# The last supertile's PSUM copies in two pairs of banks, each pair with a store of its own

## The chip, the cores and the metric

One core of a Trainium2 chip. The metric is the device time of one execution in microseconds (us), lower is better. Beside it I use the span of a profiled execution, which is 1.7 us shorter than its time wherever both are on record, and the **tail**: the end of the span minus the start of ScalarE's first copy of the last supertile. Tails are worked out from the trace's records, which carry more digits than the page. Engine names in the profile: PE is TensorE, DVE is VectorE, ACT is ScalarE, SPq is SyncE's queue. PSUM is the memory that TensorE writes its sums to; a bank is here one of the four parts of 512 numbers that the kernel's tile `ps` has in each partition. SBUF holds the other tiles. A packet is a piece that one of the 16 DMA engines moves at a time, and the backlog is what earlier stores have left for them to do.

## The reference

A depthwise convolution with a 1x1 kernel is a scaling of the channels; the pointwise convolution behind it is a matrix product.

```python
# x: (1, 384, 384, 384), dw: (1, 1, 384), pw: (384, 384), all bfloat16
out = x * dw[0, 0]
return einsum('bhwc,cd->bhwd', out, pw)
```

So it is a product of 147,456 x 384 by 384 x 384, with 113 MB read and 113 MB written.

## The kernel before

The rows are worked through in 288 supertiles of 512 rows. VectorE transposes a supertile, TensorE multiplies it into four PSUM banks, ScalarE copies the banks to an output tile in bfloat16, SyncE stores the tile in chunks of up to 10 supertiles. Towards the end the chunks get small: 4, 2, 1 and 1 supertiles.

```python
    head, tail = [[1, 1, 2, 2, 4]], [[6, 4], [4, 2, 1, 1]]
    ...
        def store(t):
            ...
            else:
                dst = rows.rearrange("(m q) d -> m (q d)", q=4)
            nc.sync.wait_ge(s_a[je % 2], je // 2 + 2)
            if je + 1 == NS:
                nc.sync.wait_ge(s_d, 1)
            nc.sync.dma_start(dst, src).then_inc(s_o[g % NR], 16)
    ...
            nq = 4
            if jj + 1 == NS:
                nq = 2
                nc.vector.wait_ge(s_o[g % NR], 16 * sum(map(len, groups[g % NR : g : NR])))
                e = nc.vector.tensor_copy(Ov[:, nq:4, j, :], PS[s][:, nq:4, :D])
                e._wait_ge(s_pe, 2 * jj + 2)
                e.then_inc(s_d)
            a = nc.scalar.copy(Ov[:, 0:nq, j, :], PS[s][:, 0:nq, :D])
            a._wait_ge(s_pe, 2 * jj + 2)
            a.then_inc(s_a[s])
```

In the last supertile alone VectorE, which has nothing left to transpose, copies banks 2 and 3 while ScalarE copies 0 and 1. One store of 393,216 bytes follows; each partition writes 3072 consecutive bytes.

## Time and profile before

| | before |
|---|---|
| time, median of 3 runs | 575.4 us (575.3 to 575.55) |
| span of the profiled run | 573.39 us |
| start of the last supertile's copies | 568.67 us |
| tail | 4.72 us |

TensorE is busy for 99% of the span, and one supertile takes it 1.95 us. The only part that this change can reach is the tail: two copies, one store, its landing, the program's end. The prediction below shows the lines and how to read them. What one does with the tail: take the times of the last copies and of SyncE's issue from the timeline, then look at the DMA share in slices of 0.1 us, to see whether the DMA engines wait for the store or the store for them.

### The profile page before, as it was taken

What the parts mean: (1) busy time and instruction counts of PE and PEld (TensorE: products, weight loads), DVE (VectorE), ACT (ScalarE), POOL (GpSimd) and SP (SyncE); (2) the same over time, 40 slices, a digit from 0 to 9 for tenths busy, and PEclk for the clock granted to TensorE, in tenths of its full rate; (3) what the DMA queues carried; (4) which work ended last, traced back from release to release, by engine and by line L of the source; (5) the groups of instructions that cost most, each with busy time, mean ns of one, the idle gap of its engine ahead of it and who ended that gap; (6) DMA issues with size and microseconds to landing.
All of it is one profiled execution on the core that took longest, in us unless ns stands there. A gap on an engine that the chain in (4) does not pass through costs nothing.

```text
span 573.4 us, 29717 instructions
## 1 busy us (share of the span) xinstructions
PE 566.5 (99%) x13869; PEld 414.7 (72%) x13869; DVE 506.7 (88%) x583; ACT 419.0 (73%) x296; POOL 0.9 (0%) x8
## 2 busy tenths in 40 slices
PE   8999999999999999999999999999999999999996
PEld 5777777777777777777777777777777777777774
DVE  7898889889889888988988988898898898889884
ACT  6777777777777777777777777777777777777775
POOL 0000000000000000000000000000000000000000
PEclk9999999999999999999999999999999999999999
DMA  9999999999999999999999999999999999998676
GB/s 363 420 340 434 417 425 432 445 414 422 428 414 425 387 400 427 392 408 390 430 392 385 404 425 401 396 416 421 399 392 411 418 387 393 422 401 364 267 288 233
DMA packets 25253, 226.88 MB, mean 396 GB/s; under 512 B 1178, under 2 KB 5147, under 8 KB 21403
## 3 DMA queue, kind: packets, MB, share of 16 engines
q1 hardware_dynamic: 24064, 225.61, 97.0%
q10 hardware_dynamic: 1178, 1.18, 0.6%
q14 instruction: 10, 0.07, 0.0%
q8 instruction: 1, 0.02, 0.0%
HBM read 113.54 MB, written 113.25 MB: 396 GB/s over the span
## 4 chain that ended last, share of the span: by engine, by line
PE 99%; ACT 0%; DVE 0%; issue 0%; POOL 0%; POOLq 0%; SPq 0%
PE ps L183 98%; PE ps L200 0%; ACT w_r L289 0%; DVE O L322 0%; PE ps L233 0%; POOL zero L249 0%; POOL warm L248 0%; PE ps L215 0%; POOLq L358 0%; SPq L103 0%
## 5 line engine op out<-in xcount | busy, mean ns | idle before, releaser
L183 PE MATMUL ps<-w_r,T 32*128 32x384 bf16 x13824 | 561.8, 321 | 0.7 <-ACT w_r L289 0.7
L276 DVE STREAM_TRANSPOSE T<-X 128x384 uint32<-128x384 uint32 x572 | 500.0, 876 | 56.0 <-DMA X<-in_x_dram 0.3
L325 ACT CAST O<-ps 128x1536 bf16<-128x1536 f32 x288 | 413.8, 1437 | 147.6 <-PE ps L183 147.6
L183 PEld LDWEIGHTS ps<-w_r,T 32*128 32x128 bf16 x13824 | 412.9, 93 | 149.4 <-issue 0.9
L289 ACT CAST w_r<-ps 128x768 bf16<-128x768 f32 x5 | 3.6, 818 | 1.0 <-PE ps L233 1.0
L200 PE MATMUL ps<-zero 32*128 32x384 bf16 x24 | 2.6, 494 | 1.4 <-POOL zero L249 1.4
L276 DVE STREAM_TRANSPOSE T<-Xl 128x384 uint32<-128x384 uint32 x4 | 3.5, 876 | 0.4
L322 DVE CAST O<-ps 128x768 bf16<-128x768 f32 x1 | 1.0, 958 | 3.0 <-PE ps L183 3.0
L261 ACT ACT_TABLE_LOAD x1 | 1.3, 1283 | 1.9 <-issue 1.9
L200 PEld LDWEIGHTS ps<-zero 32*128 32x128 bf16 x24 | 0.7, 99 | 2.6 <-issue 2.6
L233 PE MATMUL ps<-pw_n,sel_w 64*128 64x384 bf16 x18 | 2.2, 403 | 0.0
L233 PEld LDWEIGHTS ps<-pw_n,sel_w 64*128 64x128 bf16 x18 | 1.0, 114 | 1.3 <-issue 0.7
L294 DVE TENSOR_REDUCE sel<-eye 128x64 f32<-128x128 bf16 x1 | 0.3, 290 | 1.8 <-POOL eye L251 1.8
L289 DVE CAST w_r<-ps 128x768 bf16<-128x768 f32 x1 | 1.0, 958 | 0.9 <-PE ps L233 0.9
L304 DVE TENSOR_SCALAR sel_w<-sel,dw_f 128x256 bf16<-128x256 f32 x3 | 0.9, 350 | 0.0
L301 DVE COPY dw_f<-ps 128x3 f32<-128x3 f32 x1 | 0.2, 160 | 0.8 <-PE ps L215 0.8
L215 PEld LDWEIGHTS ps<-ones,dw_row 1*128 1x128 bf16 x3 | 0.2, 100 | 0.2 <-issue 0.2
L251 POOL TENSOR_SCALAR_AFFINE_SELECT eye<-ones 128x128 bf16<-128x128 bf16 x1 | 0.3, 292 | 0.1
L261 ACT COPY warm<-warm 128x1 f32<-128x1 f32 x2 | 0.3, 188 | 0.0
L249 POOL MEMSET zero<- 128x192 uint32 x1 | 0.3, 258 | 0.0
L215 PE MATMUL ps<-ones,dw_row 1*128 1x1 bf16 x3 | 0.2, 160 | 0.0
L250 POOL MEMSET ones<- 128x128 bf16 x1 | 0.2, 204 | 0.0
(5 smaller groups left out, 0.5 us busy)
## 6 DMA issues: line engine op xcount, KB each, us to landing
X<-in_x_dram SPq DMA_DIRECT2D x26, 3840.0 KB, 21.8
out_dram<-O SPq DMA_DIRECT2D x26, 3840.0 KB, 27.4
X<-in_x_dram SPq DMA_DIRECT2D x3, 1536.0 KB, 18.3
out_dram<-O SPq DMA_DIRECT2D x3, 1536.0 KB, 8.1
X<-in_x_dram SPq DMA_DIRECT2D x3, 768.0 KB, 7.2
out_dram<-O SPq DMA_DIRECT2D x3, 768.0 KB, 12.9
X<-in_x_dram SPq DMA_DIRECT2D x1, 2304.0 KB, 19.9
out_dram<-O SPq DMA_DIRECT2D x1, 2304.0 KB, 11.7
```

The source lines that it names most:

```text
L183: mm = nc.tensor.matmul(PS[s][:, q, :D], lhsT=Ts[s][32 * q : 32 * q + 32, b, par::2], rhs=w_r[32 * q : 32 * q + 32, b, par, :], start=(b, ...
L200: nc.tensor.matmul(PS[0][:, i, :D], lhsT=zero[32 * i : 32 * i + 32, 0:P], rhs=zero[32 * i : 32 * i + 32, :], start=True, stop=True, tile_p ...
L215: mm = nc.tensor.matmul(PS[1][:, 0, D + k : D + k + 1], lhsT=dw_row[:, P * k : P * k + P], rhs=ones[0:1, 0:1], start=True, stop=True,)
L233: mm = nc.tensor.matmul(PS[(k + 1) % 2][:, 2 * r + v, :D], lhsT=sel_w[64 * v : 64 * v + 64, k, r, :, :].rearrange("p q w -> p (q w)"), rhs ...
L249: nc.gpsimd.memset(zero[:].bitcast(U32), 0).then_inc(s_zero)
L251: nc.gpsimd.affine_select(out=eye[:], in_=ones[:], pattern=[[-1, P]], compare_op=mybir.AluOpType.is_equal, fill=0.0, base=0, channel_multi ...
L261: c = nc.scalar.copy(warm[:, s + 1 : s + 2], warm[:, 0:1])
L276: ins = nc.vector.transpose(out=Tw[:, 3 * h : 3 * h + 3], in_=Xw[:, :, j, 96 * h : 96 * h + 96].rearrange("p k (b w) -> p b k w", w=32),)
L289: o = nc.vector.tensor_copy(out, in_) if e == 0 else nc.scalar.copy(out, in_)
L304: nc.vector.tensor_scalar_mul(sel_w[:, k], sel[:].unsqueeze(2).to_broadcast([P, 2, 4, 32]), dw_f[:, k : k + 1]).then_inc(s_sw)
L322: e = nc.vector.tensor_copy(Ov[:, nq:4, j, :], PS[s][:, nq:4, :D])
L325: a = nc.scalar.copy(Ov[:, 0:nq, j, :], PS[s][:, 0:nq, :D])
```

## The change

Its intent: get the first half of the last supertile on its way before the second half has been copied.

```diff
+            if je + 1 == NS:
+                for k in range(2):
+                    part = slice(2 * D * k, 2 * D * k + 2 * D)
+                    nc.sync.wait_ge(s_a[je % 2], je // 2 + 2 + k)
+                    nc.sync.wait_ge(s_d, k + 1)
+                    nc.sync.dma_start(dst[:, part], src[:, part]).then_inc(s_o[g % NR], 16)
+                return
             nc.sync.wait_ge(s_a[je % 2], je // 2 + 2)
-            if je + 1 == NS:
-                nc.sync.wait_ge(s_d, 1)
             nc.sync.dma_start(dst, src).then_inc(s_o[g % NR], 16)
 ...
-            nq = 4
             if jj + 1 == NS:
-                nq = 2
                 nc.vector.wait_ge(s_o[g % NR], 16 * sum(map(len, groups[g % NR : g : NR])))
-                e = nc.vector.tensor_copy(Ov[:, nq:4, j, :], PS[s][:, nq:4, :D])
-                e._wait_ge(s_pe, 2 * jj + 2)
-                e.then_inc(s_d)
-            a = nc.scalar.copy(Ov[:, 0:nq, j, :], PS[s][:, 0:nq, :D])
+                nc.vector.wait_ge(s_pe, 2 * jj + 2)
+                nc.scalar.wait_ge(s_pe, 2 * jj + 2)
+                for q in (0, 2):
+                    nc.scalar.copy(Ov[:, q, j, :], PS[s][:, q, :D]).then_inc(s_a[s])
+                    nc.vector.tensor_copy(Ov[:, q + 1, j, :], PS[s][:, q + 1, :D]).then_inc(s_d)
+                continue
+            a = nc.scalar.copy(Ov[:, :, j, :], PS[s][:, :, :D])
```

(Cut: the final wait counts one store more.)

## The prediction

> **What bounds the kernel now.** I read four views in this order: the page (what is busy over the whole span), the chain of work that ended last, the timeline of the last five microseconds, and the DMA traffic in slices of a tenth of a microsecond there. The change touches only the last of 288 supertiles, so everything turns on what follows the last matmul.
>
> From the page, busy times and the by-engine shares of the chain:
>
> ```profile
> PE 566.5 (99%) x13869; PEld 414.7 (72%) x13869; DVE 506.7 (88%) x583; ACT 419.0 (73%) x296; POOL 0.9 (0%) x8
> PE 99%; ACT 0%; DVE 0%; issue 0%; POOL 0%; POOLq 0%; SPq 0%
> ```
>
> TensorE is busy for 99% of the span. The chain in order of time (start, length, what) ends so:
>
> ```profile
> 6.84 561.80 PE ps L183 x13824
> 568.65 0.02 issue
> 568.67 0.96 DVE O L322
> ```
>
> The matmuls run without a break from 6.84 to 568.65 us, and the changed lines touch none of their operands before the last supertile. The span ends at 573.4, so 573.39 - 568.65 = 4.74 us lie behind the last matmul. That is 0.8% of 575.4: if the change removed the whole tail it would still not be 2%. The tail on the timeline (start, length), then SyncE's own waits from 568 us on:
>
> ```profile
> 568.67 0.80 ACT L325 CAST O<-ps 128x768 bf16<-128x768 f32 x1 [0.51 <-PE ps L183]
> 568.67 0.96 DVE L322 CAST O<-ps 128x768 bf16<-128x768 f32 x1 [3.02 <-PE ps L183]
> 569.72 0.34 SPq L139 DMA_DIRECT2D out_dram<-O  x1
> ...
> SPq L158 <- DMA out_dram<-O: 2.0, 1, 2.0
> SPq L139 <- ACT O L325: 1.6, 1, 1.6
> ```
>
> The two copies start together; VectorE ends last, at 569.63. SyncE issues the store at 569.72, 0.09 us later, and is done with issuing at 570.06. It then waits 2.0 us for the landing, until about 572.1; the remaining 1.3 us to 573.4 is the program's end, which no part of the change touches. What are the DMA engines doing meanwhile? Columns: stretch, length, five engines' busy times, TensorE clock, DMA share, GB/s.
>
> ```profile
> 570.20:570.30 0.10, 0.00 (x0) 0.00 (x0) 0.00 (x0) 0.00 (x0) 0.00 (x0) 1.00 0.99 399
> 570.30:570.40 0.10, 0.00 (x0) 0.00 (x0) 0.00 (x0) 0.00 (x0) 0.00 (x0) 1.00 0.28 93
> 570.40:570.50 0.10, 0.00 (x0) 0.00 (x0) 0.00 (x0) 0.00 (x0) 0.00 (x0) 1.00 0.03 0
> 570.50:570.60 0.10, 0.00 (x0) 0.00 (x0) 0.00 (x0) 0.00 (x0) 0.00 (x0) 1.00 0.56 215
> 570.60:570.70 0.10, 0.00 (x0) 0.00 (x0) 0.00 (x0) 0.00 (x0) 0.00 (x0) 1.00 0.96 369
> ...
> 571.50:571.60 0.10, 0.00 (x0) 0.00 (x0) 0.00 (x0) 0.00 (x0) 0.00 (x0) 1.00 0.49 185
> 571.60:571.70 0.10, 0.00 (x0) 0.00 (x0) 0.00 (x0) 0.00 (x0) 0.00 (x0) 1.00 0.04 0
> ```
>
> This is the view that decides. Until 570.3 the DMA engines are still full with the store of the supertile before (a backlog: two earlier stores kept them at about full share from 563.5 on). Then there is a hole, then the last store runs at full rate until about 571.6. The hole is (1 - 0.28) + (1 - 0.03) + (1 - 0.56) = 1.73 slices of 0.1 us, so **0.17 us**. The first bytes of the last store move some 0.8 us after its issue began at 569.72. So the last store's start is set by the copies, but only just: had it been issued 0.2 us earlier, it would have stood in line behind the backlog.
>
> **What the Trainium skill says.** "DMA: Bandwidth & Descriptors", section "Latency and other measured facts": about 600 ns to the first byte for a transfer issued from SyncE or ScalarE. The trace has 0.8 us from the start of the issue, of which 0.34 is the issue itself; I use 0.84. The same page, section "Queues, rings and completion order": on each DMA engine descriptors of one issuer's ring are consumed in ring order. Both halves and the store before them come from SyncE, so an early half can at best follow the backlog without a hole. "VectorE: DVE Perf Modes", section on the TRN2 errata: from PSUM a copy of FD elements costs 120 + FD cycles at 0.96 GHz on VectorE and 172 + FD at 1.2 GHz on ScalarE, 525 and 463 ns for 384. The trace's own rows decide below and come out slightly longer. "PSUM — Partial Sum Buffer", section on bank collisions: two engines may read at once if their banks differ. Before and after, ScalarE and VectorE always hold different banks (0 and 1, then 2 and 3, of the four), so I expect neither an error nor a slowdown; the trace shows both copies at the durations that they have elsewhere.
>
> **The change part by part.** The matmuls, the other 287 supertiles and the order of instructions there stay; the listing of instructions per engine shows only two 384-wide copies for one 768-wide on ScalarE and on VectorE, and two stores for one.
>
> *Copies.* ScalarE took 1439 ns for 1536 elements and 799 for 768: 640/768 = 0.833 ns an element and 159 ns fixed, so 384 take 479 ns. VectorE took 958 for 768 and 160 for three elements from PSUM (the tiny copy of dw_f), so 1.04 an element and 157 fixed: 384 take 557 ns. Copies of one engine overlap by their fixed part: the three 348 ns VectorE operations of 256 elements at the start of the kernel fill 0.88 us, a pitch of (0.88 - 0.35)/2 = 0.265, and ScalarE's three weight copies fill 2.21 us at 817 each, a pitch of 0.70 for 768 elements, so 0.06 above the pure element time. So the second pair starts 0.40 (VectorE) and 0.38 (ScalarE) after the first. The wait for the matmuls is now an instruction of its own; I give it 0.03 us. First pair done: 568.70 + 0.56 = 569.26. Second: 568.70 + 0.40 + 0.56 = 569.66, against 569.63 before.
>
> *Stores.* Half A is issued at 569.26 + 0.09 = 569.35, 0.37 us earlier than the one store. SyncE is busy with it for 0.34, to 569.69, which is just when the second pair ends; with two waits of about 0.05 each, half B is issued near 569.80, 0.08 us later than the one store was. With 0.84 us of lead, A could move from 570.19 and B from 570.64.
>
> *DMA engines.* At 570.19 they still hold the backlog, so A follows it directly at about 570.4. The hole of 0.17 us is gone. A's 196,608 bytes take about 0.5 us, to 570.9, so B (ready at 570.64) follows A without a hole too. But the halves go in runs of 1536 bytes a partition instead of 3072. The trace has both sizes: the store of the next-to-last chunk but one moved in 1536-byte runs, the one after it in 3072:
>
> ```profile
> 567.30:569.30 2.00, 1.33 (x35) 0.72 (x24) 0.63 (x1) 1.49 (x2) 0.00 (x0) 1.00 1.04 377
> ...
> 569.50:570.30 0.80, 0.00 (x0) 0.00 (x0) 0.13 (x1) 0.00 (x0) 0.00 (x0) 1.00 0.99 396
> ```
>
> 393,216 bytes take 1.043 us at 377 GB/s and 0.993 at 396: **0.05 us** lost.
>
> *Sum.* -0.17 (hole) + 0.05 (shorter runs) = **-0.12 us** on the end of the last byte; landing (last byte to the end of SyncE's wait, some 0.4 us) and program end are as before. The 0.37 us by which A is earlier mostly goes into standing behind the backlog. Time: 575.4 - 0.12, about 575.3.
>
> **The rivals.** First, the full intent: nothing stands in front of half A, and the last byte follows B's issue only. B ready at 570.64 plus 0.52 us of bytes gives 571.16 instead of 571.6, so -0.45 us, 574.95. Against it speaks the full DMA share up to 570.3. Second, half B's issue becomes the end: if issuing two stores back to back cost more than the 0.34 us seen, or the waits on two semaphores did, B might only start at 571.1, after a new hole; then the end is 571.1 + 0.52 = 571.6, no gain, 575.4. Against it: SyncE's consecutive issues in the trace are 344 and 345 ns long. To get worse than before by even 0.3 us B would have to be issued at 570.4, 0.7 us after A's issue ended. Third, the backlog itself shifts by chance, since stores before it drain a little faster or slower against other traffic; that alone moves the hole between 0 and about 0.3 us and would hide the effect. None of the rivals reaches a per cent.
>
> **Range and chances.** Three runs before spread over 0.25 us, and executions of one kernel otherwise agree within 0.3%. An effect of -0.12 us (0.02%) is under the spread. I predict 575.3 us; the range, 574.8 to 575.8, takes the full intent less a little at the bottom and a set of runs 0.4 us slower at the top. Within 2%: 0.99. Faster and slower by over 2% need something that the tail of 4.74 us cannot give, and get 0.005 each.
>
> **What would show it.** Right: four 384-wide copies of 0.48 and 0.56 us, the pairs ending near 569.26 and 569.66 us; two SyncE issues about 0.45 us apart, the first at 569.35; no hole in the DMA share around 570.4; the last byte near 571.5 and SyncE's last wait shorter than 2.0 us (about 1.8, as it also starts 0.08 later). Wrong: a hole before half A (then the backlog was not what held it), a hole between A and B (the second rival), matmuls that end at a time other than 568.65 us by over 0.2 us (then something outside the tail moved), or a time outside 574.8 to 575.8.

## The result, and the profile after

| | before | after |
|---|---|---|
| time, median of 4 runs | 575.41 us (575.30 to 575.55) | 575.15 us (574.97 to 575.58) |
| ratio | 1 | 0.9996, interval 0.9982 to 1.0010 |
| span of the profiled run | 573.39 us | 573.86 us |
| start of the last copies | 568.67 us | 569.29 us |
| tail | 4.72 us | 4.58 us |

A ratio is the mean time of one kernel's fast runs over that of the other's of the same rounds, so not quite the ratio of the medians.

By the time the change is within noise. The profile tells more, and at first sight contradicts: the profiled run of the changed kernel has the longer span. The table says why: its tail is 0.14 us shorter, but its last copies start 0.61 us later (by the records' further digits). That lateness does not come from the tail, nor from the loop. Following ScalarE's output copies through both traces, the first one starts at 9.02 us before and at 9.64 after, and the difference is 0.61 us at the first, at the 97th and at the 277th supertile. The whole 0.61 us arose before the first supertile was finished, in code that the change does not touch. So I compare tails, and come back to the start in the last experiment.

The timeline of the tail after (start, length), then SyncE's waits in it:

```profile
569.29 0.86 ACT L329 CAST O<-ps 128x384 bf16<-128x384 f32 x2 [0.51 <-PE ps L189]
569.36 1.02 DVE L330 CAST O<-ps 128x384 bf16<-128x384 f32 x2 [3.09 <-PE ps L189]
570.00 0.85 SPq L141 DMA_DIRECT2D out_dram<-O  x2
...
SPq L164 <- DMA out_dram<-O: 1.7, 1, 1.7
SPq L144 <- ACT O L332: 1.6, 1, 1.6
SPq L140 <- DVE O L330: 0.8, 1, 0.8
```

The first store is issued 0.71 us after the copies' start (570.00 - 569.29), against 1.05 before (569.72 - 568.67); the second, by the trace's records, 1.17 us after it. SyncE's last wait is 1.7 us instead of 2.0. The DMA share in the stretch that answers to the hole before (0.61 us later), and at the end of the last store:

```profile
570.80:570.90 0.10, 0.00 (x0) 0.00 (x0) 0.00 (x0) 0.00 (x0) 0.00 (x0) 1.00 1.06 430
570.90:571.00 0.10, 0.00 (x0) 0.00 (x0) 0.00 (x0) 0.00 (x0) 0.00 (x0) 1.00 0.78 292
571.00:571.10 0.10, 0.00 (x0) 0.00 (x0) 0.00 (x0) 0.00 (x0) 0.00 (x0) 1.00 1.11 384
571.10:571.20 0.10, 0.00 (x0) 0.00 (x0) 0.00 (x0) 0.00 (x0) 0.00 (x0) 1.00 0.91 323
571.20:571.30 0.10, 0.00 (x0) 0.00 (x0) 0.00 (x0) 0.00 (x0) 0.00 (x0) 1.00 1.11 399
...
572.00:572.10 0.10, 0.00 (x0) 0.00 (x0) 0.00 (x0) 0.00 (x0) 0.00 (x0) 1.00 0.46 154
572.10:572.20 0.10, 0.00 (x0) 0.00 (x0) 0.00 (x0) 0.00 (x0) 0.00 (x0) 1.00 0.02 0
```

The share scatters about 1 (a packet is booked in the slice where it starts, so single slices read above and below), but there is no hole: both halves follow the backlog without a gap. The last byte has moved 2.87 us after the copies' start, against 3.01 before; from there to the end it is 1.70 us in both.

### The profile page after: what moved, and what is told of

Same layout as the page of the kernel before. It is cut to its first block, busy times and chain, and to the rows that moved or that the text cites. A ratio compares the mean times of both kernels' runs of the same rounds, so it can differ in the third digit from the quotient of the medians.

```text
span 573.9 us, 29721 instructions
## 1 busy us (share of the span) xinstructions
PE 567.8 (99%) x13869; PEld 383.5 (67%) x13869; DVE 508.0 (89%) x584; ACT 419.1 (73%) x297; POOL 0.9 (0%) x8
## 3 DMA queue, kind: packets, MB, share of 16 engines
q10 hardware_dynamic: 1178, 1.18, 0.6%
## 4 chain that ended last, share of the span: by engine, by line
PE 99%; DVE 0%; issue 0%; POOL 0%; POOLq 0%; DVEq 0%; SPq 0%
PE ps L189 98%; PE ps L239 1%; PE ps L206 0%; DVE O L330 0%; POOL zero L255 0%; POOL warm L254 0%; PE ps L221 0%; POOLq L365 0%; DVEq L326 0%; SPq L103 0%
## 5 line engine op out<-in xcount | busy, mean ns | idle before, releaser
L189 PEld LDWEIGHTS ps<-w_r,T 32*128 32x128 bf16 x13824 | 381.5, 93 | 181.0 <-issue 0.7
```

The source lines that it names most:

```text
L189: mm = nc.tensor.matmul(PS[s][:, q, :D], lhsT=Ts[s][32 * q : 32 * q + 32, b, par::2], rhs=w_r[32 * q : 32 * q + 32, b, par, :], start=(b, ...
```

## The experiments

My theory: the hole ahead of the last store is what the change closes, for the price of shorter runs. The rivals: the tail scatters by chance; the split copies themselves save time; two transfers are faster than one. Times without a ratio come from single runs, whose state is unknown; tails are compared across them because the loop keeps its pace of 1.95 us a supertile in every trace looked at and the tail repeats, as the first two runs show. In the diffs, `-` and `+` are against the changed kernel unless said otherwise.

**1 and 2. Both kernels once more, unedited.**

> The kernel before, unedited, to learn how far a profile repeats. I measure the tail: end of the span minus the start of ScalarE's last copy (of the first one, where there are two). Before 4.72 us, after 4.58. Theory (hole): the tail is set by the store queue, so it repeats within 0.05 us: 4.67 to 4.77, with a hole in the DMA share of about 0.17 us ahead of the last store; the span differs from 573.39 only by what happens ahead of the first supertile, up to 0.6 us. Rival (backlog by chance): the earlier stores drain differently each time, and the tail scatters by 0.15 us or more, so that the 0.14 us between before and after could be chance.

> The changed kernel, unedited. Theory (hole): tail 4.53 to 4.63 us again, no hole in the DMA share, and the pace of the loop, one supertile in 1.95 us, is as before; in the time a ratio of 0.9995 to 1.0000. Rival (chance): a tail anywhere from 4.5 to 4.8. Second rival (the copies got quicker or slower): the second pair of copies ends at a place other than 1.10 us after the start of the first.

Measured: tails 4.72 and 4.57 us; so each repeats within 0.005 us, and chance is out (a third pair, in experiments 11 and 12 and on another chip, agrees). The span of the kernel before was 0.97 us longer than in the first profile, more than the 0.6 allowed for, and all of it had arisen before the first output copy (9.99 us against 9.02). The second pair of copies ends 1.09 us after the start of the first, as in the first profile. But the times: 576.08 (one run) for the kernel before, and for the changed kernel 575.25, median of 5 (575.05 to 575.61), against 575.21, median of 9, ratio 1.0001 (0.9988 to 1.0015), where 0.9995 to 1.0000 was expected. A saving of 0.14 us is 0.02%, and the times scatter by 0.5 us.

**3. The split copies with one store.**

```diff
-                for k in range(2):
-                    part = slice(2 * D * k, 2 * D * k + 2 * D)
-                    nc.sync.wait_ge(s_a[je % 2], je // 2 + 2 + k)
-                    nc.sync.wait_ge(s_d, k + 1)
-                    nc.sync.dma_start(dst[:, part], src[:, part]).then_inc(s_o[g % NR], 16)
+                nc.sync.wait_ge(s_a[je % 2], je // 2 + 3)
+                nc.sync.wait_ge(s_d, 2)
+                nc.sync.dma_start(dst, src).then_inc(s_o[g % NR], 16)
```

(Cut: the final wait counts one store less again.)

> The four copies of the change, but one store as before, after all four. Theory (hole): the store is issued about 1.18 us after the copies' start instead of 1.05, because two copies on one engine end later than one; the hole grows by as much to about 0.3 us, tail 4.85 us (4.80 to 4.90), worse than both kernels. Rival (the copies are what saves): 4.58 as in the changed kernel.

Measured: tail 4.85 us (time of the one run 575.74). Issue at 570.36, 1.18 us after the copies' start:

```profile
569.18 0.86 ACT L327 CAST O<-ps 128x384 bf16<-128x384 f32 x2 [0.51 <-PE ps L187]
...
570.36 0.34 SPq L139 DMA_DIRECT2D out_dram<-O  x1
```

The hole, in the same columns as before:

```profile
570.80:570.90 0.10, 0.00 (x0) 0.00 (x0) 0.00 (x0) 0.00 (x0) 0.00 (x0) 1.00 0.28 93
570.90:571.00 0.10, 0.00 (x0) 0.00 (x0) 0.00 (x0) 0.00 (x0) 0.00 (x0) 1.00 0.03 0
571.00:571.10 0.10, 0.00 (x0) 0.00 (x0) 0.00 (x0) 0.00 (x0) 0.00 (x0) 1.00 0.00 0
571.10:571.20 0.10, 0.00 (x0) 0.00 (x0) 0.00 (x0) 0.00 (x0) 0.00 (x0) 1.00 0.08 31
571.20:571.30 0.10, 0.00 (x0) 0.00 (x0) 0.00 (x0) 0.00 (x0) 0.00 (x0) 1.00 0.96 369
```

It is one slice and a bit longer than before, and the tail is 0.13 us longer, which is the delay of the issue (1.18 - 1.05). With a hole ahead of it, the start of the last store follows its issue one for one. The split copies alone cost time.

**4. The copies of before with two stores**, ScalarE's half first.

```diff
-                    nc.sync.wait_ge(s_a[je % 2], je // 2 + 2 + k)
-                    nc.sync.wait_ge(s_d, k + 1)
+                    if k == 0:
+                        nc.sync.wait_ge(s_a[je % 2], je // 2 + 2)
+                    else:
+                        nc.sync.wait_ge(s_d, 1)
...
-                for q in (0, 2):
-                    nc.scalar.copy(Ov[:, q, j, :], PS[s][:, q, :D]).then_inc(s_a[s])
-                    nc.vector.tensor_copy(Ov[:, q + 1, j, :], PS[s][:, q + 1, :D]).then_inc(s_d)
+                nc.scalar.copy(Ov[:, 0:2, j, :], PS[s][:, 0:2, :D]).then_inc(s_a[s])
+                nc.vector.tensor_copy(Ov[:, 2:4, j, :], PS[s][:, 2:4, :D]).then_inc(s_d)
```

> The two copies of before (ScalarE banks 0 and 1, VectorE 2 and 3), but two stores: the first after ScalarE's copy alone, the second after VectorE's. Theory (hole): the first half is issued about 0.9 us after the copies' start and can move 0.84 us later, at 1.73, as the backlog ends (1.65 to 1.80), so the hole closes all but some hundredths: tail 4.57 to 4.65. Then the splitting of the copies bought nothing. Rival (the early pair is needed): the first half comes after the backlog's end with a hole of 0.1 us or more, tail 4.68 to 4.72.

Measured: tail 4.59 us (575.0 for the one run). The first half is issued 0.82 us after the copies' start instead of 0.71, and of the hole one slice of 0.66 is left:

```profile
570.20:570.30 0.10, 0.00 (x0) 0.00 (x0) 0.00 (x0) 0.00 (x0) 0.00 (x0) 1.00 1.01 399
570.30:570.40 0.10, 0.00 (x0) 0.00 (x0) 0.00 (x0) 0.00 (x0) 0.00 (x0) 1.00 0.66 231
570.40:570.50 0.10, 0.00 (x0) 0.00 (x0) 0.00 (x0) 0.00 (x0) 0.00 (x0) 1.00 1.06 369
```

So of the 0.14 us, 0.12 come from the second store alone; pairing the banks adds 0.02, no more than the moment of the last byte varies among the three profiles with the changed ending (2.87 to 2.90 us after the copies' start, 2.89 here). ScalarE's half ends earlier than VectorE's anyway, and that was head start enough.

**5. Two stores, both held until all four copies are done.**

```diff
-                    nc.sync.wait_ge(s_a[je % 2], je // 2 + 2 + k)
-                    nc.sync.wait_ge(s_d, k + 1)
+                    nc.sync.wait_ge(s_a[je % 2], je // 2 + 3)
+                    nc.sync.wait_ge(s_d, 2)
```

> The change's copies and two stores, but both stores wait for all four copies. Tail measured as end of the span minus the start of ScalarE's first copy of the last supertile; one store after four copies had 4.85 us. Theory (the saving is the early issue of the first half, and halves themselves cost a little): the first half is issued 1.18 us after the copies' start, moves from about 2.02, the second follows without a hole, and the run of two times eight short packets an engine takes 0.05 us more than eight long ones: tail 4.86 to 4.92. Rival (two transfers are quicker by themselves): below 4.82.

Measured: tail 4.93 us (575.52), a little over the range. The first issue lies 1.18 us after the copies' start, the same as in experiment 3, so the two differ only in one store against two halves: **0.085 us is the price of the halves**. Two transfers are not faster by themselves. The two lines to set beside those of experiment 3:

```profile
568.87 0.86 ACT L329 CAST O<-ps 128x384 bf16<-128x384 f32 x2 [0.51 <-PE ps L189]
...
570.05 0.82 SPq L141 DMA_DIRECT2D out_dram<-O  x2
```

By the trace's records a 3072-byte packet takes about 0.124 us on its DMA engine and a 1536-byte one 0.067, more than half. The last supertile's 8 or 16 packets an engine so take 8 x 0.124 = 0.99 or 16 x 0.067 = 1.07 us, which is nearly all of it.

**6 to 8. A shorter backlog.** The last supertiles are grouped 2, 2, 2, 1, 1 instead of 4, 2, 1, 1, so that the earlier stores start sooner. Done to the kernel before, to the changed kernel, and to experiment 4:

```diff
-    head, tail = [[1, 1, 2, 2, 4]], [[6, 4], [4, 2, 1, 1]]
+    head, tail = [[1, 1, 2, 2, 4]], [[6, 4], [2, 2, 2, 1, 1]]
```

> The kernel before with the last supertiles grouped 2, 2, 2, 1, 1 instead of 4, 2, 1, 1, so that the store queue is some 0.2 to 0.3 us less behind when the last store comes. Theory (the last store is started by its own issue): tail 4.72 us as before, only the hole ahead of it grows to 0.3 us or more. Rival (the backlog holds the last store in the kernel before as well): tail 4.45 to 4.6.

> The changed kernel with the same grouping. Theory (in the changed kernel the backlog holds the first half, by 0.1 to 0.25 us): both halves move earlier, the first from about 1.55 us after the copies' start, the last byte about 0.25 us earlier than in the changed kernel: tail 4.28 to 4.38, thus 0.35 to 0.4 less than the kernel before. In the time: 0.9990 to 1.0000, as the start of the kernel scatters by up to a microsecond. Rival (half B's own issue, 1.17 us after the copies' start, already sets the end): tail 4.55 to 4.6.

> The two unsplit copies with two stores (ScalarE's half first), with the same grouping. Theory (splitting the copies is worth nothing behind the backlog and 0.1 us without it, as the first half is issued 0.87 instead of 0.76 us after the last matmul): tail 4.40 to 4.46, about 0.1 more than with split copies. Rival (something later sets the end in both): equal within 0.03.

Measured: tails 4.69, 4.48 and 4.57 us. For the first two the direction is the theory's: the kernel before hardly moves (its store starts with its own issue), the changed kernel gains 0.10 us (its first half stood behind the backlog). Of these gains 0.02 and 0.03 us lie behind the last byte, though, from which it is 1.68 us to the end here instead of 1.70; the last byte itself comes 0.01 us earlier in the kernel before and 0.07 in the changed one. The sizes of the last two were missed, 4.28 to 4.38 and 4.40 to 4.46 being expected. For the changed kernel the reason is the backlog: I had expected it to end 0.2 to 0.3 us sooner, and by the trace's records its last packet ended only 0.06 to 0.09 us sooner (1.72 to 1.74 us after the copies' start instead of 1.78 to 1.82). For experiment 4 it is not: its last byte does not come earlier at all (2.91 us after the copies' start, 2.89 before), because its first half, issued at 0.82 us, had only just reached the backlog and now has a hole ahead of it again. The 0.10 us between split and unsplit copies came as expected. Time of the changed kernel so grouped: 575.13, median of 6, against 575.25, ratio 0.9998 (0.9985 to 1.0010). The other two, single runs: 575.79 and 575.23.

**9 and 10. Hardly any backlog left**: the same with 2, 2, 1, 1, 1, 1, for the changed kernel and for experiment 4.

> The changed kernel with the last supertiles grouped 2, 2, 1, 1, 1, 1, so that the store queue is empty earlier: the grouping 2, 2, 2, 1, 1 freed it only 0.09 us earlier and brought a tail of 4.48 us where I had expected 4.28 to 4.38. Theory (the backlog holds the first half until about 1.6 us after the copies' start, then its own issue does, 0.71 + 0.84): a little hole ahead of the first half; the last byte about 1.2 us after that, tail 4.40 to 4.48. Rival (no backlog at all is worth what my prediction called the full intent): tail 4.2 to 4.3.

> The unsplit copies with two stores, ScalarE's half first, with the grouping 2, 2, 1, 1, 1, 1. Theory (without a backlog the tail follows the issue of the first half, 0.11 us later than with split copies): tail 0.08 to 0.14 us above that of tail1_after. Rival: equal within 0.03.

Measured: tails 4.46 and 4.54 us (575.25 and 575.08, single runs). Now the first half of the changed kernel has a hole ahead of it again:

```profile
570.30:570.40 0.10, 0.00 (x0) 0.00 (x0) 0.00 (x0) 0.00 (x0) 0.00 (x0) 1.00 0.69 277
570.40:570.50 0.10, 0.00 (x0) 0.00 (x0) 0.00 (x0) 0.00 (x0) 0.00 (x0) 1.00 0.13 31
570.50:570.60 0.10, 0.00 (x0) 0.00 (x0) 0.00 (x0) 0.00 (x0) 0.00 (x0) 1.00 0.12 46
570.60:570.70 0.10, 0.00 (x0) 0.00 (x0) 0.00 (x0) 0.00 (x0) 0.00 (x0) 1.00 0.77 276
```

Its copies start at 569.04 in this run and the first store is issued at 569.75, so bytes move again 0.8 us after the issue. With the DMA engines waiting for it, the split of the copies is worth 0.085 us here. This is the smallest tail I found, 0.26 us below the kernel before, and not the 4.2 to 4.3 us of the rival; the limit is no longer the queue but the first half's own way through copy and issue. By the times it can't be told from the others.

**11 and 12. A start of fixed length.** The times scatter by more than the tail saves, and the traces say that the scatter lies before the first supertile. So I lengthened that start on purpose: VectorE does its first reduction 26 times in a chain while TensorE runs 18 idle rounds instead of 3. Done to both kernels, the same edit:

```diff
-        idle_work(3)          # the second of the two
+        idle_work(18)
...
-        nc.vector.tensor_reduce(... sel ...).then_inc(s_dwf)
+        for n in range(TIMER):             # 26
+            r = nc.vector.tensor_reduce(... sel ...)
+            if n:
+                r._wait_ge(s_tm, n)
+            r.then_inc(s_tm if n + 1 < TIMER else s_dwf)
```

> The kernel before with a longer start of fixed length: VectorE repeats the small reduction 26 times in a chain, so that the weights are made some 8 us later, while TensorE keeps busy with idle matmuls, so that it has reached its full rate before any of its work counts. In the profiles so far the first output copy of the loop starts between 9.02 and 10.0 us, later where the matmuls stay slow for longer, and the loop and the tail repeat within hundredths. Theory (the scatter of the times comes from that start alone): the times of these runs lie within 0.15 us of one another instead of 0.4 to 0.6, some 7 to 8 us above 575.3. Rival (the scatter is elsewhere, ahead of or behind the span): they scatter as before.

> The changed kernel with the same longer start. Theory: as narrow, and its median is 0.14 us (0.08 to 0.20) below that of fixed_before, the saving that the tails show (4.72 against 4.58). Rival (the saving of the tail does not reach the time): no difference, within 0.05 us.

Measured:

| | times, us | median | tail |
|---|---|---|---|
| start fixed, kernel before | 581.77, 581.80, 581.81, 582.31 | 581.80 | 4.71 |
| start fixed, changed kernel | 581.66, 581.67, 581.68, 581.69 | 581.67 | 4.58 |
| unedited kernel before, same rounds | 575.23 to 576.13 (7 runs) | 575.57 | |

Now the last copies begin at the same time in both:

```profile
575.34 0.80 ACT L331 CAST O<-ps 128x768 bf16<-128x768 f32 x1 [0.51 <-PE ps L185]
575.34 0.96 DVE L328 CAST O<-ps 128x768 bf16<-128x768 f32 x1 [3.01 <-PE ps L185]
576.38 0.34 SPq L141 DMA_DIRECT2D out_dram<-O  x1
```

```profile
575.35 0.86 ACT L335 CAST O<-ps 128x384 bf16<-128x384 f32 x2 [0.51 <-PE ps L191]
575.42 1.02 DVE L336 CAST O<-ps 128x384 bf16<-128x384 f32 x2 [3.09 <-PE ps L191]
576.06 0.85 SPq L143 DMA_DIRECT2D out_dram<-O  x2
```

The changed kernel's four times lie within 0.03 us of each other, three of the four of the kernel before within 0.04, and the medians differ by 0.13 us, against 0.14 between the tails. The saving is real and reaches the time. One run, 582.31 at a granted clock of 0.997 against 0.999 to 1.0, stands apart, so that the expected 0.15 us was missed for the kernel before; it wasn't profiled, and what it met is open. As ratios to the unedited kernel before the two are 1.0111 (1.0094 to 1.0127; it includes the run of 582.31) and 1.0105 (1.0088 to 1.0122); the start costs 6 us (7 to 8 were expected) and is no version to use.

What differs from run to run in the unedited start? The weights' 18 matmuls, the first line from the page of before, the second from the page after:

```profile
L233 PE MATMUL ps<-pw_n,sel_w 64*128 64x384 bf16 x18 | 2.2, 403 | 0.0
```

```profile
L239 PE MATMUL ps<-pw_n,sel_w 64*128 64x384 bf16 x18 | 3.1, 521 | 0.0
```

The same work took 2.2 us in one run and 3.1 in the other: TensorE reached its full rate at a different moment. By the traces' records its granted clock (the share of full speed that TensorE is allowed) rose to full at 5.19 us in the one and at 7.93 in the other. With the fixed start it had risen by 6.6 us, the weights' matmuls began at 10.8, and their mean is 323 ns in both kernels. That is not all of it. In the second run of the kernel before, the one with the latest start (first output copy at 9.99 us), the mean was 490 ns, and VectorE waited for the first input:

```profile
DVE T L276 <- DMA X<-in_x_dram: 1.1, 1, 1.1
```

So at least two things scatter there, the moment of the full rate and the landing of the first load. The long start covers both, and how much each contributes was not told apart.

## Why the prediction was right

- **What the time says.** By itself little. The range of 574.8 to 575.8 us also holds the times of the first two rivals (574.95 and 575.4), and the 0.26 us between the medians is nearly twice what the tails show; in experiment 2 the medians lay the other way round. That the mechanism was the predicted one is read from the profiles and the experiments.
- **Bound and limit.** "4.74 us lie behind the last matmul", so no effect near 2%: held. All of the change's effect is in the tail.
- **Copies.** ScalarE's were right (0.479 and 0.484 us, second starting 0.376 after the first, 0.38 predicted). VectorE's were right in length (0.558 and 0.548) but not in pitch: 0.474 us instead of 0.40. The overlap of two operations had been taken from ones within SBUF, while these read PSUM; that this is the reason was not tested. VectorE's separate wait cost 0.07 us, not 0.03; ScalarE's cost nothing that shows. The second pair so ended 1.09 us after the copies' start instead of 0.99. It cost nothing, because half B stood in line behind half A.
- **Stores.** Issues at 0.71 and 1.17 us after the copies' start; 0.68 and 1.13 predicted. The second issue took 0.395 us instead of 0.345. No hole between the halves: the second rival fell. That half A stands in line behind the backlog fits too: its first packet starts 1.66 us after the copies' start, and 1.55 in experiment 9, where hardly any backlog is left, from an issue at 0.71 us in both.
- **The hole.** Predicted 0.17 us, in truth about 0.23: so much the DMA engines lack on average between 1.4 and 2.5 us after the copies' start when each packet of the trace's records is spread over its own duration (0.230; 0.226 and 0.231 in the other two profiles with this ending). I summed three slices; the slice at 570.60 lacks 0.04 and the next one, not shown there, another 0.14, which makes 0.19:

```profile
570.70:570.80 0.10, 0.00 (x0) 0.00 (x0) 0.00 (x0) 0.00 (x0) 0.00 (x0) 1.00 0.86 338
```

  The rest is hidden, because a slice books a packet whole where it starts. A hole's ragged edges belong to it: by the records the share falls from full to nothing over about 0.15 us, and it rises as slowly.
- **The price of shorter runs.** Predicted 0.05 us from the rates of long stretches, measured 0.085 (experiments 3 and 5). The rate over a stretch of 2 us in the middle of other traffic understated it; the mean packets named in experiment 5 give 0.08.
- **The sum.** -0.17 + 0.05 = -0.12 predicted; -0.23 + 0.085 = -0.145 from the corrected terms; -0.14 measured in the tails. The first term was too small by a quarter, the second by two fifths, and the errors nearly cancelled: that the sum was better than its parts was luck. The records of the two first profiles say the same without the experiments: from the copies' start to the last byte the DMA engines' idle time fell by 0.235 us and the time of their packets grew by 0.093, which is the 0.142 us by which the last byte came earlier.
- **The first rival, the full intent** (-0.45 us), was held back by the backlog as argued, but not by it alone: with the backlog all but gone the tail is 0.26 us below the kernel before, not 0.45. The estimate let half B run 0.84 us after its own issue; but half A's bytes, themselves starting 0.8 us after their issue, run on past that moment.
- **A slip.** Half B issued at 570.4 would by the prediction's own terms end at 570.4 + 0.84 + 0.52 = 571.76 us, 0.16 later than before and not 0.3. Nothing hung on it.
- **The third rival**, a backlog that shifts by chance by up to 0.3 us, was wrong: the tail repeats within 0.006 us in three profiles of each kernel's ending, on two chips (its last byte within 0.03). The scatter that hides the effect is at the other end of the kernel. My check "matmuls that end at a time other than 568.65 by over 0.2 us" would have called the prediction wrong for a reason that has nothing to do with the change.

## What to carry to other kernels

Before splitting the last store, look in slices of 0.1 us at what the DMA engines do when it is issued. Here the gain was at most the hole ahead of the store, and it came from the earliest issue that reached the backlog; finer copies paid, by 0.085 to 0.10 us of tail, only where the backlog had been shortened. Splitting transfers has its own price (here 0.085 us), and splitting the copies without the store only lost (0.13 us). When a change is worth less than the scatter of the times, compare the stretch of the trace that it touches, and if the time must show it, fix whatever scatters.

## What the Trainium skill lacked or had wrong

- "VectorE: DVE Perf Modes": its errata section has 120 + FD cycles for a copy of FD elements from PSUM on VectorE and 172 + FD on ScalarE, an estimate of 525 and 463 ns for 384 elements; the trace has 548 to 558 and 479 to 484.
- "DMA: Bandwidth & Descriptors", "Latency and other measured facts": about 600 ns to the first byte, without saying from where it counts. Here bytes moved 0.8 us after the start of the issue, about 0.5 after its end. The page has no measured figure for a trn2 store in shorter runs: 393,216 bytes as two transfers of 1536-byte runs cost 0.085 us more than as one of 3072.
- "TensorE: Matmul & The Clock Gate", "What you observe", has the full rate come about 4 us into sustained matmul activity, and that moment vary by 500 ns either way from run to run. In the twelve profiles with the unedited start the first matmul began at 1.43 us, and the first one of under 340 ns came between 4.85 and 8.05 us, a spread of 3.2 us.
